# Nine equal chunks of 512 tokens in place of ten uneven ones, for windowed attention followed by a feed-forward layer

## The chip, the core and the metric

The kernel runs on one core of one Trainium2 chip. The core has five engines that run side by side, each with its own instruction list in program order: TensorE (PE in the profile; its weight loads are listed as PEld), VectorE (DVE), ScalarE (ACT), GpSimd (POOL) and SyncE (SP), which here issues the DMA transfers. Matrix products are accumulated in PSUM, everything else lies in SBUF. The metric is the device time of one execution in microseconds, as the median of the runs.

## The reference

Eight batches of eight heads, 576 positions and head size 64 go through causal attention in a window of 128 positions, with a distance penalty that has a slope of its own per head. The result, 4608 tokens of 512 numbers, goes through two matrix products with a piecewise function between them.

```python
scores = scale * np.matmul(q, k.transpose(0, 1, 3, 2))
rel = pos[:, None] - pos[None, :]
mask = (rel >= 0) & (rel < window)                    # window = 128
scores = np.where(mask, scores + bias[None], -1000000000.0)
attn = np.exp(scores - np.max(scores, axis=-1, keepdims=True))
attn = attn / (np.sum(attn, axis=-1, keepdims=True) + 1e-09)
x = np.matmul(attn, v)                                # to (4608, 512)
h = x @ w_in                                          # (512, 2048)
g = np.where(h >= 1, h, np.where(h <= -1, 0.0, (h + 1) ** 2 / 4))
return g @ w_out                                      # (2048, 512)
```

The two weight matrices arrive as 64-bit floats. The kernel makes 32-bit floats of them on the chip.

## The kernel before

**Chunks and stages.** The 36 blocks of 128 tokens are worked off in ten chunks (`SIZES`, ten numbers: 2, eight times 4, 2). For each chunk there is an attention stage, eight heads one after the other, and a feed-forward sweep over eight groups `g`; group `g` makes the hidden columns `g` and `8+g`, each of 128. While the sweep of chunk c runs, the attention of chunk c+1 is woven into it.

**Attention of one head** (`scores`, `weights_t`, `values`): products of queries and keys into PSUM tiles `s` (L544, L548 with plain float32; L550, L551 with operands split in two), then on DVE a selection by distance (L557) and a pass that adds the penalty and takes the row's bound (L560), on ACT the exponential (L564), on DVE or ACT the division by the row's sum (L575, L573), on PE the transposition `p` (L591), a copy to SBUF on ACT or DVE, on POOL two triangular selections per tile (L607, L610 or L622, L625), on PE the products with v into `x` (L659) and the copy into `xn`. Heads of chunks below `LIGHT` = 3 use plain float32 on PE; the others split q, k, v and the weights of attention into a rounded part and a rest of type fp32r, and multiply the parts.

**The feed-forward sweep.** Products in fp32r take three matmuls per pair of operands: high by high, high by rest, rest by high. In chunks 1 to 8 the first layer uses seven products of half-size quarters in place of eight (`PRODUCTS`, L722), with sums S1 to S4 of the weights' quarters A11 to A22 and differences T of the tokens' quarters. `build` (L387) splits each such operand once, during chunk 1, and writes it to DRAM; `fetch` (L397) reads it back in later chunks into a ring of ten buffers. The sums S are made by `operand` on POOL or, where the planner likes it better, on DVE (L380, L381). Chunk 9, of two blocks, uses eight plain products. The nonlinear function (`nonlinear`, L729) is a clamp on DVE, a square on ACT and a maximum on DVE, then a rounding on ACT (L744) and a rest on DVE (L745). The second layer (`layer2`) adds three fp32r matmuls per block and hidden column into `acc` (L762 to L764).

**Chunk 0** has a sweep of its own (`first_sweep`): both layers run in plain float32 on PE (L918 and L757), with weights just converted. During it the 32 halves of the weights are read and converted (`fetch_raw`, `convert`: two passes on ACT, L345 and L355, and two on DVE, L350 and L358), and split for later (`split_out`).

**What sets the order.** All operations are recorded first with their dependences. `Plan.schedule` (L119) is a list scheduler: it simulates the five engines with a table of costs and takes, on each engine, the ready operation that is due first; due times (`deadlines`) come from the order in which PE's operations were recorded. `emit` then writes the instructions in the planned order, so each engine's list is fixed when the kernel is built. Buffers with one slot in the pools (`buf`) add dependences: a tile that takes over a slot waits for the last use of the one before. The output tiles `o` have two slots.

Of the kernel before, what the change touches and what calls it, by code (L numbers as in the profile page):

```python
# [31 lines left out]
RAW_IN = ("B11", "B21", "T2", "T1", "B22", "T3")  # L32


class Buf:


    def __init__(self, name, make, before):
        self.name, self.make, self.before, self.tile = name, make, before, None
        self.nodes, self.writers, self.readers = [], {}, {}  # L40
        self.over = False
# [8 lines left out]
class Node:  # L50
    def __init__(self, alts, deps):
        self.alts, self.deps = alts, deps
        self.next, self.late, self.start, self.end, self.eng = [], None, None, None, None


class Plan:


    CROSS, SAME = 0.09, 0.04

    def __init__(self):
        self.nodes, self.slots, self.turn = [], {}, {}

    def buf(self, pool, tag, n, shape, dtype, name):
        k = self.turn.get(tag, 0)
        self.turn[tag] = k + 1
        slot = f"{tag}{k % n}"
        b = Buf(name, lambda: pool.tile(shape, dtype, name=name, tag=slot), self.slots.get(slot))
        self.slots[slot] = b
        return b  # L70

    def op(self, alts, reads=(), writes=()):
# [24 lines left out]
        for b, _ in reads + writes:  # L97
            b.nodes.append(node)
# [6 lines left out]
    def deadlines(self):  # L105
# [5 lines left out]
        for n in reversed(self.nodes):  # L111
            late = n.nominal if "PE" in n.alts else t + 5.0
            for s in n.next:
                late = min(late, s.late - min(a[1] for a in n.alts.values()) - self.CROSS)
# [3 lines left out]

    def schedule(self, engines, bandwidth):  # L119
        self.deadlines()  # L120
        free = {e: 0.0 for e in engines}
# [5 lines left out]
        tick = 0  # L127

# [18 lines left out]
        while events:  # L147
# [3 lines left out]
            cands = [(n.late, n.index, n, r) for n, r in avail[e] if r <= t + 1e-9]  # L151
# [3 lines left out]
            pick = None  # L155
            for late, _, n, r in cands:
                busy = n.alts[e][0]
                worse = [(m, q) for m, q in avail[e] if q > t + 1e-9 and q < t + busy - 0.05 and m.late < late - 0.2
# [8 lines left out]
            if pick is None:  # L167
                wake(e, min(q for _, q in avail[e] if q > t + 1e-9))
                continue
            n = pick  # L170
# [37 lines left out]
def windowed_attention_then_ffn(  # L208
# [14 lines left out]
    P = 128  # L223
# [4 lines left out]
    SIZES = [2] + [4] * 8 + [2]  # L228
# [6 lines left out]
    LIGHT = 3  # L235
    FIRST = 2
# [31 lines left out]

    def pool(t, f):
# [14 lines left out]
    half = const.tile([P, 1], F32, name="half")  # L284
    G.memset(half, 0.5)
    loaded = const.tile([P, 1], F32, name="loaded")
    S.activation(loaded, half, AF.Exp)
# [39 lines left out]
    def convert(i):
        fc, n = WEIGHTS[i]
        r = raw.pop(i)
        if fc not in w_of:  # L330
            w_of[fc] = buf("wp", "w", NFC + 1, [P, 2, DM], F32, f"w{fc}")
        w = w_of[fc]
# [7 lines left out]
        def o():  # L340
            return w.t[:, n].bitcast(I32)
# [15 lines left out]
        plan.op(dve_fast(DM, shift), [(r, 1)], [(w, n)])  # L357
        plan.op(dve(DM, lambda: V.tensor_tensor(o(), o(), low(), ALU.add), True), [(r, 0), (w, n)], [(w, n)])  # L358

    def split_out(fc):  # L360
        f = w_of[fc]
        w = wo_of[fc] = buf("wp", "w", NFC + 1, [P, 2, DM], F32R, f"wo{fc}")
        plan.op(act(DM, lambda: S.copy(w.t[:, 0], f.t[:, 1])), [(f, 1)], [(w, 0)])
        plan.op(dve(DM, lambda: V.tensor_tensor(w.t[:, 1], f.t[:, 1], w.t[:, 0].bitcast(F32), ALU.subtract), True),
                [(f, 1), (w, 0)], [(w, 1)])
# [3 lines left out]
    def operand(g, name):  # L369

        if name[0] == "A":
            w = w_of[g if name[1] == "1" else NG + g]
            k0 = 0 if name[2] == "1" else 2
            return w, 0, lambda: w.t[:, 0, k0 * P:(k0 + 2) * P].rearrange("p (c f) -> p c f", c=2)
        if (g, name) not in sums_w:
# [33 lines left out]
    def load_qk(p):  # L409
# [11 lines left out]
        other = c < LIGHT and p % 2  # L421
# [3 lines left out]
        kr = buf("ap", "kk" if other else "kr", 1, [P, 2, 5 * P], F32, f"kr_{p}")  # L425
        if c < LIGHT:
            st["kr"] = (kr, None, lambda: kr.t[:, 0])
            plan.op(dma(P * (n + P) * 4, lambda: DMA.dma_start(kr.t[:, 0, :n + P], k[rows, t0 - P:t0 + n])), (), [kr])
            return
        st["kr"] = (kr, None, lambda: kr.t[:, :, :n + P])  # L430
        for r in lo_rows:
            plan.op(dma(P * (n + P) * 4, lambda r=r: DMA.dma_start(
                kr.t[r, :, :n + P], k[rows, t0 - P:t0 + n].rearrange("(j d) t -> d j t", j=2))), (), [(kr, r.start)])

    def load_v(p):
        c, g = divmod(p, NPAIR)
        nb, b0 = SIZES[c], STARTS[c]
        if c == 0:
            if g % 2 == 0:
                t = pair[p]["v2"] = buf("ring", "r", 10, [P, 2, nb, P], F32, f"vn_{p}")  # L440
            else:
                t = pair[p - 1]["v2"]
            pair[p]["vn"] = (t, g % 2, lambda: t.t[:, g % 2])
            plan.op(dma(P * nb * 512, lambda: DMA.dma_start(t.t[:, g % 2], v[g, :, :nb])), (), [(t, g % 2)])
            return
        if c < LIGHT and p % 2:
            t = buf("ap", "vs", 1, [P, 2, 5, P], F32, f"vn_{p}")
            pair[p]["vn"] = (t, None, lambda: t.t[:, 0])
# [6 lines left out]
    def prepare_q(p):  # L455
# [3 lines left out]
        if c == 0:  # L459
            ql = buf("ring", "r", 10, [P, 2, n], F32, f"ql_{p}")  # L460
# [5 lines left out]
        for j in range(2):  # L466
            if c < LIGHT:
                plan.op(act_fn(n, lambda j=j: S.activation(ql.t[:, j, :n], qr(), AF.Copy, scale=qscale[:, g, j:j + 1])),
                        [(b, key)], [(ql, j)])
# [13 lines left out]
    def prepare_k(p):  # L483
# [4 lines left out]
        b, key, kr = pair[p]["kr"]  # L488
        kk = pair[p]["kk"] = buf("ap", "kk", 1, [P, 2, 5 * P], F32R, f"kk_{p}")
        kl = pair[p]["kl"] = buf("ap", "kl", 1, [P, 2, 5 * P], F32R, f"kl_{p}")  # L490
        for j in range(2):
            plan.op(act(n, lambda j=j: S.copy(kk.t[:, j, :n], kr()[:, j])), [(b, key)], [(kk, j)])
            plan.op(dve(n, lambda j=j: V.tensor_tensor(kl.t[:, j, :n], kr()[:, j], kk.t[:, j, :n].bitcast(F32),
                                                       ALU.subtract), True), [(b, key), (kk, j)], [(kl, j)])
# [18 lines left out]
    def att_bank(c, name):  # L513
        turn[0] += 1
        if c < FIRST and turn[0] % 2:
            return bank("acc1", 2, name)
        return bank("pa", 2, name)

    def scores(m, blks):
# [4 lines left out]
        if m not in head:  # L524
            z = buf("fp", "sw", 4, [P, 2, P], F32, f"z_{m}") if c == 0 else buf("ap", "z", 2, [P, 4, P], F32, f"z_{m}")
# [478 lines left out]
```

## Time and profile before

| What | us |
|---|---|
| median of 3 runs (1008.35 to 1009.16) | 1008.95 |
| the profiled execution | 1009.93 |
| its span from first to last instruction | 1008.1 |
| PE busy in it | 995.6 |
| DVE / ACT / POOL busy in it | 798.4 / 709.9 / 209.6 |
| data moved by DMA | 198.04 MB |

The page cuts the span into 40 slices of 25.2 us. PE is busy 9 tenths or more in every slice but the first (7) and the last (8). DVE has 6 tenths in the first slice, 8 or 9 in the next nine, 7 to 9 up to the 33rd, and falls after that; ACT has 9 in the second slice and 6 to 8 in nearly all others up to the 35th. From 230 us to 860 us the profile repeats every 105 us, which is one chunk of four blocks. In the tables below, a matmul that reads plain float32 is listed as two instructions, so 64 such matmuls show as x128.

### The profile page before, as it was taken

The page shows a single profiled execution, that of the slowest core. Times are in us where ns is not written, and L with a number is a line of the kernel's source. Part 1 is how long each engine was busy: PE and PEld are TensorE (multiplying, and loading weights), DVE is VectorE, ACT ScalarE, POOL GpSimd, SP SyncE. Part 2 cuts the span into 40 slices and gives each one's busy share as a digit, 9 for nine tenths or more (in the row PEclk, how much of TensorE's full clock was granted, in tenths as well). Part 3 has the DMA queues.
Part 4 walks back from the last instruction along what each step waited for, and adds up shares of the span by engine and source line. Part 5 has one row for each costly group of instructions (what it writes and reads, how often), then busy time and mean ns, then how long its engine had stood idle before and what let it go on. Part 6 is the DMA issues. An engine that isn't in the chain of part 4 may idle for free.

```text
span 1008.1 us, 19663 instructions
## 1 busy us (share of the span) xinstructions
PE 995.6 (99%) x6432; PEld 896.5 (89%) x6432; DVE 798.4 (79%) x2102; ACT 709.9 (70%) x1827; POOL 209.6 (21%) x319
## 2 busy tenths in 40 slices
PE   7999999999999999999999999999999999999998
PEld 6777799999999999999999999999999999999897
DVE  6899898999777987798779877897789778766443
ACT  7987788767777776777777777777778666754433
POOL 3231133403211221122112211121122221211000
PEclk9899999999999999999999999999999999999999
DMA  8596356567766677658664966576667655764471
GB/s 293 178 353 232 94 191 206 182 208 203 219 189 186 186 232 189 185 172 261 190 187 155 270 175 188 184 235 182 193 195 219 195 169 180 220 196 151 122 229 63
DMA packets 101909, 198.04 MB, mean 196 GB/s; under 512 B 11312, under 2 KB 14896, under 8 KB 101808
## 3 DMA queue, kind: packets, MB, share of 16 engines
q1 hardware_dynamic: 101808, 196.78, 64.3%
q8 instruction: 52, 0.85, 0.3%
q14 instruction: 49, 0.40, 0.1%
HBM read 170.52 MB, written 26.21 MB: 195 GB/s over the span
## 4 chain that ended last, share of the span: by engine, by line
PE 98%; ACT 1%; DVE 0%; issue 0%; POOL 0%; POOLq 0%; ACTq 0%
PE hA L722 18%; PE hB L722 14%; PE acc L762 13%; PE acc L763 13%; PE acc L764 12%; PE x L659 9%; PE p L591 3%; PE s L548 3%; PE h L918 3%; PE acc L757 3%; PE s L550 2%; PE s L551 2%; PE h L722 2%; PE idle L932 0%; PE s L544 0%
## 5 line engine op out<-in xcount | busy, mean ns | idle before, releaser
L762 PE MATMUL acc<-wo,gh 128*128 128x512 f32 x544 | 219.6, 404 | 0.0
L763 PE MATMUL acc<-wo,gh 128*128 128x512 f32 x544 | 214.6, 395 | 0.0
L764 PE MATMUL acc<-wo,gl 128*128 128x512 f32 x544 | 213.3, 392 | 0.0
L622 POOL TENSOR_SCALAR_AFFINE_SELECT lu<-lu 128x512 fp32r<-128x512 f32 (+1 forms) x112 | 79.6, 710 | 578.4 <-ACT lu L615 571.0
L735 ACT ACTIVATE m<-m,half 128x512 f32<-128x512 f32 (+1 forms) x160 | 108.6, 679 | 39.7 <-DVE m L732 24.6
L564 ACT ACTIVATE z<-z,nmax 128x128 f32<-128x128 f32 x288 | 112.7, 393 | 25.3 <-DVE nmax L560 25.1
L764 PEld LDWEIGHTS acc<-wo,gl 128*128 128x128 f32 x544 | 102.2, 188 | 23.6 <-DVE gl L745 0.2
L855 DVE TENSOR_TENSOR h<-hB,s 128x256 f32<-128x256 f32 x192 | 80.7, 420 | 46.9 <-PE hB L722 22.6
L762 PEld LDWEIGHTS acc<-wo,gh 128*128 128x128 f32 x544 | 102.8, 189 | 9.3 <-ACT gh L744 0.4
L763 PEld LDWEIGHTS acc<-wo,gh 128*128 128x128 f32 x544 | 103.1, 190 | 8.3
L745 DVE TENSOR_TENSOR gl<-h,gh 128x512 fp32r<-128x512 f32 x128 | 93.8, 733 | 16.8 <-ACT gh L744 15.4
L860 ACT COPY s<-hA 128x256 f32<-128x256 f32 x192 | 70.4, 367 | 49.3 <-PE hA L722 46.4
L722 PEld LDWEIGHTS hA<-x_T,w_S 128*128 128x128 f32 x672 | 93.7, 189 | 8.0
L744 ACT CAST gh<-h 128x512 fp32r<-128x512 f32 x128 | 79.2, 619 | 29.7 <-DVE h L738 28.4
L722 PE MATMUL hA<-x_T,w_S 128*128 128x256 f32 x672 | 99.2, 283 | 0.0
L738 DVE TENSOR_TENSOR h<-h,m 128x512 f32<-128x512 f32 x128 | 89.1, 696 | 2.2 <-ACT m L735 2.1
L557 DVE COPY_PREDICATED s<-older,s 128x256 f32<-128x256 uint32 x144 | 60.7, 422 | 23.4 <-PE s L551 15.6
L733 DVE TENSOR_SCALAR m<-h 128x512 f32<-128x512 f32 x128 | 55.3, 432 | 29.9 <-ACT h L866 27.5
L866 ACT COPY h<-hA 128x256 f32<-128x256 f32 x64 | 23.8, 372 | 73.6 <-PE hA L722 73.4
L560 DVE CUSTOM_DVE_ANT_0 z<-s,rel 128x128 f32<-128x128 f32 x288 | 72.2, 284 | 2.0
L625 POOL TENSOR_SCALAR_AFFINE_SELECT lu<-lu 128x512 fp32r<-128x512 f32 (+1 forms) x112 | 72.4, 669 | 0.0
L659 PEld LDWEIGHTS x<-lu,vs 128*128 128x128 f32 x528 | 67.5, 189 | 1.9
(127 smaller groups left out, 2169.4 us busy)
## 6 DMA issues: line engine op xcount, KB each, us to landing
w_S<-d_S SPq DMA_DIRECT2D x224, 256.0 KB, 2.7
w_A<-d_A SPq DMA_DIRECT2D x200, 256.0 KB, 3.0
kr<-in_k_dram SPq DMA_DIRECT2D x57, 320.0 KB, 4.8
vn<-in_v_dram SPq DMA_DIRECT2D x33, 320.0 KB, 3.3
out_dram<-o SPq DMA_DIRECT2D x36, 256.0 KB, 4.0
qr<-in_q_dram SPq DMA_DIRECT2D x33, 256.0 KB, 4.7
raw<-in_moe_w_in_dram SPq DMA_DIRECT2D x16, 512.0 KB, 6.0
raw<-in_moe_w_out_dram SPq DMA_DIRECT2D x16, 512.0 KB, 5.2
```

Source lines behind the costliest of these rows:

```text
L564: plan.op({"ACT": (0.385, 0.48, lambda i=i: S.activation(z.t[:, i], z.t[:, i], AF.Exp, bias=nmax.t[:, i:i + 1], scale=-1.0, accum_out=sm.t ...
L622: G.affine_select(out=lu.t[:, s, 0:2 * nb:2], in_=a.bitcast(F32), pattern=[[0, nb], [-1, P]], base=0, channel_multiplier=1, compare_op=ALU ...
L659: T.matmul(px[:, q0 * P:q1 * P], sv, mv.rearrange("p a w -> p (a w)"), start=(w == 0), stop=(w == len(todo) - 1), skip_group_check=True)
L722: T.matmul(o.t[:, :2 * P], w.t[:, a, kb], x.t[:, b, kb], start=start and n == 0, stop=stop and n == len(todo) - 1, skip_group_check=True)
L735: plan.op(act_fn(n, lambda: S.activation(m.t[:, :n], m.t[:, :n], AF.Square, bias=half[:, 0:1], scale=0.5)), [m], [m])
L738: plan.op(dve(n, lambda: V.tensor_tensor(f.t[:, :n], h.t[:, :n], m.t[:, :n], ALU.max), not h_ps), src + [m], dst)
L744: plan.op(act(n, lambda: S.copy(gh.t[:, :n], f.t[:, :n])), dst, [gh])
L745: alts = dve(n, lambda: V.tensor_tensor(gl.t[:, :n], f.t[:, :n], gh.t[:, :n].bitcast(F32), ALU.subtract), True)
L762: T.matmul(a.t, gh.t[:, ts], w.t[:, 0], start=first, stop=False)
L763: T.matmul(a.t, gh.t[:, ts], w.t[:, 1], start=False, stop=False)
L764: T.matmul(a.t, gl.t[:, ts], w.t[:, 0], start=False, stop=last)
L855: plan.op(dve(2 * P, lambda: V.tensor_tensor(f.t[:, key * 2 * P:(key + 1) * 2 * P], b.t[:, :2 * P], s.t, ALU.add)), [b, s], [(f, key)])
```

## The change

The tokens are cut into nine chunks of four blocks. Chunk 0 becomes a full chunk: its attention (eight heads of four blocks, plain float32, `LIGHT` = 2) stands ahead of all feed-forward work, its first layer uses the eight plain fp32r products per group on two halves of the tokens, and its second layer uses float32 matmuls for the hidden columns of groups 0 to 5 (`WHOLE` = 6) and three fp32r matmuls for groups 6 and 7. All split operands, the sums S among them, are now built during chunk 0; the sums are made on DVE alone. Chunks 1 to 8 use the seven products. The nonlinear function takes another form: max(h+1, 0), squared after halving, and a last step min(max(h, 1), that); its first step and all roundings may go to ACT or DVE, as the planner chooses. Several one-slot buffers are split in two (`kr`, `kk`, `lu`), weight halves share a common set of 17 slots that the planner hands out, and the planner runs twelve rounds, in each of which the due times are taken from the round before (`later`), and keeps the round whose plan ends first.

```diff
-    CROSS, SAME = 0.09, 0.04
+    CROSS, SAME, BACKLOG, STRETCH, SWAP, ROUNDS = 0.09, 0.04, 4.0, 1.5, 8.0, 12
...
+        for _ in range(self.ROUNDS):
+            order = self.forward(engines, bandwidth)
+            end = max(n.end for n in order)
+            if best is None or end < best[0]:
...
+            self.later(order)
...
-    SIZES = [2] + [4] * 8 + [2]
+    SIZES = [4] * 9
...
-    LIGHT = 3
-    FIRST = 2
+    LIGHT = 2
+    FIRST = 1
+    WHOLE = 6
...
+    def rounded(n, out, src):
+
+        alts = act(n, lambda: S.copy(out(), src()))
+        alts.update(dve_fast(n, lambda: V.tensor_copy(out(), src())))
+        return alts
...
-            alts = pool(0.75, lambda: G.tensor_tensor(s.t, af(), bf(), alu))
-            alts.update(dve(2 * P, lambda: V.tensor_tensor(s.t, af(), bf(), alu), True))
-            plan.op(alts, [(ab, ak), (bb, bk)], [s])
+            plan.op(dve(2 * P, lambda: V.tensor_tensor(s.t, af(), bf(), alu), True), [(ab, ak), (bb, bk)], [s])
...
-        if c < FIRST and turn[0] % 2:
-            return bank("acc1", 2, name)
+        if c < FIRST and turn[0] % 3:
+            return bank(f"acc{turn[0] % 3 - 1}", 2, name)
...
+    def nonlinear(c, fc, h, src, f):
+
+        n, psum = 4 * P, f is not h
+        m = buf("fp", "m", 2, [P, n], F32, f"m_{c}_{fc}")
+        alts = (dve if psum else dve_fast)(n, lambda: V.tensor_scalar(m.t, h.t, 1.0, 0.0, ALU.add, ALU.max))
+        alts.update(act(n, lambda: S.activation(m.t, h.t, AF.Relu, bias=one[:, 0:1]), 0.144 if psum else 0.186))
+        plan.op(alts, src, [m])
+        plan.op(act_fn(n, lambda: S.activation(m.t, m.t, AF.Square, scale=0.5)), [m], [m])
+        dst = [f] if psum else src
+        plan.op(dve(n, lambda: V.scalar_tensor_tensor(f.t, h.t, 1.0, m.t, ALU.max, ALU.min), not psum), src + [m], dst)
...
+        if c == 0 and fc % NG < WHOLE:
+            w, g, key = fo[fc % NG], gs[c, fc], fc // NG
+            plan.op(pe(0.858, lambda: T.matmul(a.t, g.t[:, ts], w.t[:, key], start=first, stop=False)), [g, (w, key)], [a])
...
+            if c == 0 and x == "A22":
+                for name in SUMS:
+                    build(g, name)
...
+            def plain(i, tt, st=st, g=g):
...
+                for kk in range(2):
+                    w = PLAIN[2 * i + kk]
+                    product(h, have[c, g, w], xs[c, f"B{kk + 1}{tt + 1}"], kk == 0, kk == 1, 2 * tt * P)
...
+            if c == 0:
+                for i, tt in ((0, 0), (0, 1), (1, 0), (1, 1)) if g < NG - 1 else ((0, 0), (1, 0), (0, 1), (1, 1)):
+                    steps.append([lambda plain=plain, i=i, tt=tt: plain(i, tt)])
...
-    while at[0] < ready[1]:
-        emit_attention(at[0] + 1)
-        if at[0] > ready[1] // 3 and converted[0] < EARLY:
-            weights_upto(converted[0] + 1)
-    weights_upto(EARLY)
+    emit_attention(ready[1])
+    operands_upto(AHEAD)
+    for fs in tokens_ready(0).values():
+        for f in fs:
+            f()
...
-    plan.emit(tc, ("PE", "ACT", "DVE", "POOL", "SP"), 270e3)
+    plan.emit(tc, ("PE", "ACT", "DVE", "POOL", "SP"), 370e3)
```

**First place: PE where the feed-forward of chunk 0 begins.** The rows give line, operation, output tile, operand tiles, columns and count. `s_4_..` is a score tile of head 8 and on (`kr_4` is the first pair of chunk 1), `p` a transposition, `x` the products with v, `h` a hidden column. Before, the eight heads of two blocks are all done, and then float32 products on whole tokens follow:

```order
L659 MATMUL x_7_456<-gh_7_428,vn_2_166 128x128
L659 MATMUL x_7_456<-gl_7_439,vn_2_166 128x128
L659 MATMUL x_7_456<-gh_7_428,vn_2_166 128x128
L918 MATMUL h_0_0_466<-xn_0_265,w0_336 128x256 x4
L548 MATMUL s_8_0_487<-kr_4_249,ql_4_397 128x256 x2
L548 MATMUL s_8_2_502<-kr_4_249,ql_4_397 128x256 x2
L548 MATMUL s_9_2_511<-kr_4_249,ql_4_397 128x256 x2
L918 MATMUL h_0_8_524<-xn_0_265,w8_414 128x256 x4
```

In the changed kernel the same place, after eight heads of four blocks (`x_0_B21` is the quarter of the tokens that needs the last four heads, `b_0_A12` a split quarter of the weights of group 0), reads:

```order
L774 MATMUL x_7_629<-gh_7_586,vn_3_197 128x128
L664 MATMUL s_9_2_651<-kr_4_263,ql_4_340 128x256 x2
L774 MATMUL x_8_659<-lu_8_637,vn_4_324 128x128 x8
L837 MATMUL h0_0_0_577<-x_0_B21_657,b_0_A12_473 128x256 x6
L837 MATMUL h0_0_0_577<-x_0_B12_478,b_0_A11_471 128x256 x6
L707 MATMUL p_9_703<-ident_78,z_9_618 128x128 x4
L664 MATMUL s_10_0_711<-kr_5_247,ql_5_529 128x256 x2
L837 MATMUL h1_0_0_723<-x_0_B11_460,b_0_A21_646 128x256 x6
```

Scores of heads 8 and 9, and the whole of head 8, have moved ahead of the first product that needs all of chunk 0's tokens.

**Second place: ACT at the same point.** `x_0_B21` is the rounding of that quarter, `xn_0` the tokens of chunk 0, `raw` a weight half under conversion:

```order
L451 ACTIVATE raw_5_392<-raw_5_392 128x512
L782 COPY xn_0_313<-x_6_602 64x512
L720 COPY lu_8_637<-p_8_621 128x512
L680 ACTIVATE z_9_618,sum_9_641<-z_9_618,nmax_9_619 128x128 x2
L359 CAST b_0_A22_649<-w_0_429 128x256
L782 COPY xn_0_313<-x_7_629 64x512
L359 CAST x_0_B21_657<-xn_0_313 128x512
L359 CAST x_0_B22_671<-xn_0_313 128x512
```

Before, chunk 0 needed no rounding of its tokens: behind the last copy into `xn_0` ACT went on with conversions.

**Third place: the end of ACT's list.** Before, two output tiles leave the core at the end:

```order
L744 CAST gh_9_7_13231<-g_9_7_13226 128x256
L735 ACTIVATE m_9_15_13244<-m_9_15_13244,half_83 128x256
L744 CAST gh_9_15_13255<-g_9_15_13253 128x256
L769 COPY o_9_0_13265<-acc_9_0_12821 128x512
L769 COPY o_9_1_13268<-acc_9_1_12837 128x512
```

Now there are four, and the roundings `gh` of the last columns stand on DVE:

```order
L851 ACTIVATE m_8_7_13116<-m_8_7_13116 128x512
L849 ACTIVATE m_8_15_13140<-h1_8_7_13101,one_83 128x512
L851 ACTIVATE m_8_15_13140<-m_8_15_13140 128x512
L885 COPY o_8_0_13175<-acc_8_0_12445 128x512
L885 COPY o_8_1_13181<-acc_8_1_12455 128x512
L885 COPY o_8_2_13187<-acc_8_2_12469 128x512
L885 COPY o_8_3_13190<-acc_8_3_12485 128x512
```

The last two copies take over the slots of the first two.

More of the change, by code (lines that the diff above doesn't have):

```diff
@@ L31 @@
 PLAIN = ("A11", "A12", "A21", "A22")
[L32 removed]
+SUMS = ("S1", "S2", "S3", "S4")
 class Buf:
@@ L97, in op @@
         for b, _ in reads + writes:
-            b.nodes.append(node)
+            if b.tag and not b.nodes:
+                node.need = b
+            if node not in b.nodes[-1:]:
+                b.nodes.append(node)
+                node.uses.append(b)
         node.deps.discard(node)
@@ L127, in schedule, with room @@
         tick = 0
+        slots = {tag: [(0.0, i) for i in range(n)] for tag, (n, _) in self.common.items()}
+        for _, bufs in self.common.values():
+            for b in bufs:
+                b.slot, b.left, b.last = None, len(b.nodes), 0.0
+        def room(n, t):
+            b = n.need
+            if b is None:
+                return True
+            free = sum(x <= t + 1e-9 for x, _ in slots[b.tag])
+            return free > 0 and b.fits(free)
         def wake(e, t):
@@ L167, in schedule @@
             if pick is None:
-                wake(e, min(q for _, q in avail[e] if q > t + 1e-9))
+                soon = [q for _, q in avail[e] if q > t + 1e-9]
+                wake(e, min(soon + [t + 0.2] if held_back else soon))
                 continue
+            if e == "DVE" and pick.alts[e][3] and lock["POOL"] > t + 0.15:
+                for late, _, n, r in cands:
+                    if not n.alts[e][3] and late < pick.late + self.SWAP and next(iter(n.alts)) == e:
+                        pick = n
+                        break
             n = pick
@@ new lines, in tokens @@
+            def tokens(n, g=g):
+                if g == NG - 1 and c + 1 < NCHUNK:
+                    for f in tokens_ready(c + 1).get(n, ()):
+                        f()
+            def plain(i, tt, st=st, g=g):
+                if i not in st:
+                    st[i] = bank("hB" if i else "hA", 1, f"h{i}_{c}_{g}")
+                h = st[i]
+                for kk in range(2):
+                    w = PLAIN[2 * i + kk]
+                    product(h, have[c, g, w], xs[c, f"B{kk + 1}{tt + 1}"], kk == 0, kk == 1, 2 * tt * P)
+                    if tt:
+                        used(c, g, w)
+                if tt:
+                    tag = ("gh", 4) if g < WHOLE else ("h", 3)
+                    nonlinear(c, i * NG + g, h, [h], buf("fp", *tag, [P, 4 * P], F32, f"g_{c}_{i * NG + g}"))
@@ new lines, in sweep_steps @@
+            if c == 0:
+                for i, tt in ((0, 0), (0, 1), (1, 0), (1, 1)) if g < NG - 1 else ((0, 0), (1, 0), (0, 1), (1, 1)):
+                    steps.append([lambda plain=plain, i=i, tt=tt: plain(i, tt)])
+                    for n in {(1, 0): (0, 1, 3), (1, 1): (4, 5, 6)}.get((i, tt), ()):
+                        steps[-1].append(lambda tokens=tokens, n=n: tokens(n))
+                    steps += [[second]] * 2
+                steps[-1].append(lambda g=g: weights_upto(4 * g + 4))
+            else:
```

413 lines of the change are left out of this document (214 added, 199 removed).

## The prediction

> **What bounds the kernel now.** I read the page first, its busy times and the chain of work that ended last:
>
> ```profile
> PE 995.6 (99%) x6432; PEld 896.5 (89%) x6432; DVE 798.4 (79%) x2102; ACT 709.9 (70%) x1827; POOL 209.6 (21%) x319
> ...
> PE 98%; ACT 1%; DVE 0%; issue 0%; POOL 0%; POOLq 0%; ACTq 0%
> ```
>
> PE is busy for 99% of the span, and 98% of the chain is PE. So I asked in which stretch PE is not busy, with the table of busy times by stage (us of the stage, then busy us and count of each engine, granted clock, DMA share, GB/s):
>
> ```profile
> 20.00:30.00 10.00, 5.48 (x32) 4.44 (x32) 8.93 (x27) 9.52 (x24) 5.38 (x9) 0.85 0.84 284
> ...
> 60.00:90.00 30.00, 30.00 (x139) 22.33 (x138) 28.16 (x79) 25.03 (x60) 8.91 (x10) 1.00 0.95 337
> ...
> 335.00:440.00 105.00, 105.00 (x706) 96.39 (x705) 85.08 (x220) 77.22 (x199) 22.51 (x34) 1.00 0.70 199
> ```
>
> PE waits only in the first 30 us. From 60 to 90 us DVE is busy 28.16 of 30 and DMA at 0.95, and PE still misses nothing. So two things decide: how much PE work there is, and what PE loses at the start and at the very end.
>
> **PE work.** While PE never waits, the pieces of the chain give the time from one matmul to the next (start, length, what, count; a plain float32 matmul counts as two):
>
> ```profile
> 30.12 3.41 PE h L918 x8
> ...
> 36.37 1.73 PE h L918 x8
> ...
> 41.13 1.73 PE s L548 x8
> ...
> 42.85 0.86 PE acc L757 x2
> ...
> 45.01 1.78 PE x L659 x16
> ```
>
> ```profile
> 121.20 0.44 PE p L591 x4
> ```
>
> ```profile
> 385.91 0.71 PE hA L722 x6
> ...
> 388.04 0.23 PE acc L762
> ...
> 389.44 1.11 PE x L659 x10
> ```
>
> One float32 matmul of 256 columns takes 1.73/4 = 0.432, one of 512 takes 0.86, one of 128 in the values 1.78/8 = 0.2225; in fp32r, 256 columns take 0.71/6 = 0.119 and 512 take 0.232 (0.23 rounded; three in a row take 0.69 to 0.70); a transposition 0.11; the values of one split head 1.11. The float32 stage that goes:
>
> ```profile
> L918 PE MATMUL h<-xn,w 128*128 128x256 f32 x128 | 32.0, 395 | 0.0
> ...
> L757 PE MATMUL acc<-w,g 128*128 128x512 f32 x64 | 31.6, 592 | 0.0
> ```
>
> By counting both programs:
> - First layer in float32: 64 matmuls go, 64 x 0.432 = -27.7.
> - Plain products of chunk 0 come (384), those of chunk 9 go (192); the other 2688 stay: +192 x 0.119 = +22.8.
> - Second layer in float32: 32 become 48 (six groups, two columns, four blocks): +16 x 0.86 = +13.7.
> - Second layer in fp32r: 3 x 544 become 3 x 528: -48 x 0.232 = -11.1.
> - Attention: `LIGHT` falls from ten blocks to eight. 16 float32 scores (-6.9) and 32 float32 values (-7.1) go, 32 split scores (+3.8) come; eight split heads of two blocks become whole ones, 1.11 in place of about 0.64 (four matmuls of 0.1, two of 0.119): +3.8.
>
> Sum: **-8.7 us** of PE work. This is the firm term: it rests on counts and on times without a wait.
>
> **The start.** PE's first scores, and what stands around its waits (start, length, engine; in brackets the idle time before and who ended it; then two stages):
>
> ```profile
> 5.33 0.85 PE s L544 x4
> ...
> 10.54 0.71 PE s L544 x4
> ```
>
> ```profile
> 28.47 0.79 PE L659 MATMUL x<-gh,vn 128*128 128x128 f32 x2 [2.16 <-POOL gh L610]
> ```
>
> ```profile
> 21.00:24.00 3.00, 1.40 (x10) 0.95 (x8) 2.89 (x15) 2.96 (x12) 0.89 (x3) 1.00 0.73 271
> 24.00:27.00 3.00, 1.54 (x8) 1.02 (x8) 2.71 (x6) 2.98 (x7) 2.21 (x4) 1.00 0.88 265
> ```
>
> Before, PE's own work between 5.33 and the first product of the feed-forward at 30.12 is 16 x 0.355 (L544) + 8 x 0.432 + 16 x 0.11 + 24 x 0.2225 = 16.3, so 8.5 of these 24.8 us are lost: ACT is busy 2.96 and 2.98 of 3 and PE half. On top, the first eight products take 3.41 in place of 1.73, at half clock: 1.7 lost. Together 10.2.
>
> The order of the changed kernel has, ahead of the first product that needs all tokens of chunk 0 (`x_0_B21`), 64 values, 36 transpositions, 32 scores of 256, 16 of 128 and six fp32r products: 14.2 + 4.0 + 13.8 + 5.7 + 0.7 = 38.4 of PE work. PE alone would get there at 5.33 + 38.4 = 43.7. ACT's list up to the rounding of that quarter, at ACT's own times from one start to the next:
>
> ```profile
> 60.23 1.32 ACT L468 ACTIVATE ql<-qr,qscale 128x512 f32<-128x512 f32 x2
> 61.62 0.59 ACT L604 COPY gh<-p 128x512 f32<-128x512 f32 x1
> 62.10 0.51 ACT L735 ACTIVATE m<-m,half 128x256 f32<-128x256 f32 x1
> ...
> 63.08 0.69 ACT L355 ACTIVATE raw<-raw 128x512 int32<-128x512 uint32 x1
> 63.65 0.68 ACT L345 ACTIVATE raw<-raw 128x512 f32<-128x512 f32 x1
> ...
> 66.64 0.39 ACT L564 ACTIVATE z<-z,nmax 128x128 f32<-128x128 f32 x1
> ...
> 67.03 0.39 ACT L564 ACTIVATE z<-z,nmax 128x128 f32<-128x128 f32 x1
> ```
>
> From the first exponential on there are 38 exponentials at 0.39, 7 scalings of q at 0.61 (half of 1.32, less the overlap), 14 copies at 0.48, 9 conversion passes at 0.57, 3 roundings of 512 at 0.5 and 3 of 256 at 0.3 (both estimates, from the copy): 14.8 + 4.3 + 6.7 + 5.1 + 1.5 + 0.9 = 33.3. Where it began and ended before:
>
> ```profile
> 7.72 0.40 ACT L564 ACTIVATE z<-z,nmax 128x128 f32<-128x128 f32 x1 [2.33 <-DVE nmax L560]
> ...
> 30.15 0.37 ACT L667 COPY xn<-x 64x256 f32<-64x256 f32 x1 [0.55 <-PE x L659]
> ```
>
> That list of before sums to 19.4 in the same way and took 22.4, a factor of 1.155 for waits. So ACT gets to the quarter at 7.72 + 33.3 x 1.155 = 46.2, without waits at 41.0; the rest on DVE adds 0.7. I take **47**, the value nearest to the row of before; the bounds are 43.7 (PE alone) and a start that loses as much as before. The loss is then 47 - 5.3 - 38.4 = 3.3, with no stage at half clock, since PE would be busy 38.4 of 41.7 us. Gain: 10.2 - 3.3 = **-6.9**.
>
> [...]
>
> **Behind the start.** Per group of chunk 0, PE has 48 x 0.119 + 8 x 0.86 and a head of 3.9: 16.5 us. DVE's work beside it:
>
> ```profile
> L358 DVE CUSTOM_DVE_ANT_0 w<-raw,w 128x1024 uint16<-128x1024 uint16 x32 | 22.2, 696 | 0.5 <-ACT raw L355 0.2
> ...
> L350 DVE TENSOR_SCALAR w<-raw 128x512 int32<-128x512 int32 x32 | 15.9, 502 | 0.7 <-ACT raw L345 0.6
> ...
> L391 DVE TENSOR_TENSOR b_A<-w,b_A 128x256 fp32r<-128x256 f32 x32 | 15.1, 478 | 0.0
> ...
> L770 DVE COPY o<-acc 128x512 f32<-128x512 f32 x9 | 6.2, 690 | 1.4 <-PE acc L764 0.8 <-DMA out_dram<-o 0.6
> ```
>
> ```profile
> 60.15 0.42 DVE L391 TENSOR_TENSOR b_S<-S,b_S 128x256 fp32r<-128x256 f32 x1
> 60.49 0.68 DVE L358 CUSTOM_DVE_ANT_0 w<-raw,w 128x1024 uint16<-128x1024 uint16 x1
> ```
>
> Four conversions (1.2 each), eight rests (0.48), four sums (0.43, like the rests), two nonlinear steps per column (0.69 each), a head of 3.0 and some three roundings at 0.69 (no row shows a rounding on DVE; a float32 copy out of PSUM is the dearest neighbour) make 18.4 by listed durations. But a next instruction starts about 0.08 before the one before ends (60.15 to 60.49 for one of 0.42), which takes off 2.2, and part of the first steps go to ACT: 13 to 16 for 16.5. So the sums and splits hide behind PE, and POOL, relieved of the sums, is not waited for. I cost them at nothing, and at the rival's price if the cover is gone. DMA needs about 280 GB/s there; 337 passed without a wait. In all later chunks columns wait 7 us of PE work or more between their last product and their use, as before: nothing.
>
> **The end.**
>
> ```profile
> 1003.31 1.28 ACT L769 COPY o<-acc 128x512 f32<-128x512 f32 x2 [1.06 <-PE acc L764]
> ...
> 1003.57 0.40 PE L764 MATMUL acc<-wo,gl 128*128 128x512 f32 x1
> ```
>
> ```profile
> out_dram<-o SPq DMA_DIRECT2D x2, 256.0 KB, 2.0
> ```
>
> Before, the last matmul ends at 1003.97 and the span 4.1 later. Now four output tiles share two slots: the second leaves PE 1.4 ahead of the end, is copied (0.6) and lands 2.0 later, 1.3 behind PE's end; only then can the fourth be copied (0.6), land (2.0) and the program close (1.4, as before): 5.4. **+1.3.**
>
> **Sum.** 1009.93 - 8.7 - 6.9 + 1.3 = 995.6 for the profiled execution; it lay 1.0 over the median, so **994.6**.
>
> **Rivals.**
> - The clock drops once more at the start: PE waits in a changed order on new chains (POOL's selections of 512 columns). Price 1.7, as before: 996.3. Chance 0.13.
> - The start is no cheaper: PE still loses 10.2, since ACT's list is longer than assumed (DVE's rows shift roundings to it). 994.6 + 6.9 = 1001.5. For it: ACT is the engine that is full there. Chance 0.15.
> - DVE becomes the bound of chunk 0's sweep, because its instructions wait for others and lose their overlap: 18.4 - 16.5 = 1.9 for each of eight groups, +15: 1009.8. Against: 28.16 of 30 busy without a wait of PE. It begins to cost when DVE needs 1.3 times its spacing. Chance 0.10, mostly with a smaller price.
> - Slower: the loss at the start grows with the attention that stands there. Twice the blocks, twice the loss, clock included: 20.4 in place of 3.3, +17.1: 1011.7. It ends above the time before when the loss passes 19.7. For it: the chain scores, bound, exponential, division, transposition, selection, values is run through for every head with little else for PE. Against: six PSUM tiles serve it in place of four, and PE's share of the work rises. Chance 0.08.
> - The change moves nothing measurable, because new waits eat the work saved: 0.02.
>
> **How the numbers follow.** The forecast has 0.52, with its own range of 990 to 999. The range reaches from PE alone at the start and no cost at the end (994.6 - 3.3 - 1.3 = 990.0, less the spread of runs) to the start that is no cheaper with some 2 us of waits: **989.5 to 1003.5**. It leaves out most of the DVE rival and the slower one. A measurement of this kernel tells about 0.2% from no change, 2 us. Faster by more than that: 0.52 + 0.13 + 0.15 + 0.04 = 0.84; within: 0.07; slower: 0.09.
>
> **What would show it.** Right: PE's busy time near 984, first product with all tokens of chunk 0 near 47 us, a granted clock of 1.00 in every stage from 10 to 60 us, no wait of PE between 50 us and its last matmuls, a wait of the third and fourth copy of `o` for the DMA at the end. Wrong: PE idle in stages between 50 and 160 us behind DVE or ACT (third rival), or a first such product past 55 us (second and fourth).

## The result and the profile after

The changed kernel took 997.96 us (median of four runs, 997.62 to 1000.59) beside 1008.85 for the kernel before: a ratio of 0.9898, 95% interval 0.9881 to 0.9916. That is 10.9 us less; the forecast was 994.6, 14.3 less. Its profiled execution was the one of 1000.59, 2.6 us above the median, with a span of 998.8 us.

The page after, its busy times, and the chain of work that ended last, by engine and by line:

```profile
PE 985.4 (99%) x6448; PEld 884.8 (89%) x6448; DVE 809.2 (81%) x2121; ACT 652.3 (65%) x1606; POOL 186.7 (19%) x274
...
PE 82%; DVE 8%; DMA 4%; ACT 4%; issue 1%; SPq 0%; ACTq 0%; DVEq 0%
PE hA L837 18%; PE hB L837 14%; PE acc L878 12%; PE acc L879 12%; PE acc L880 12%; PE x L774 6%; DMA d_S<-b_S 4%; PE s L666 3%; PE s L667 3%; PE p L707 2%; ACT z L680 1%; DVE b_S L506 1%; DVE z L676 1%; DVE S L494 1%; DVE s L673 1%
```

PE is as full as before, yet the chain, 98% PE before, now runs through DVE, DMA and ACT for 16% of the span. One transfer stands out: `d_S<-b_S`, the write of a split sum, with 4% (some 40 us). The busy times by stage show where (columns as in the prediction):

```profile
24.00:27.00 3.00, 3.00 (x26) 2.88 (x25) 3.00 (x15) 3.00 (x13) 0.99 (x2) 1.00 1.03 406
...
60.00:90.00 30.00, 30.00 (x182) 23.82 (x181) 27.21 (x76) 26.82 (x58) 2.75 (x4) 1.00 0.85 281
90.00:120.00 30.00, 28.31 (x159) 20.82 (x158) 26.89 (x84) 21.84 (x55) 3.01 (x2) 1.00 0.83 281
120.00:160.00 40.00, 37.16 (x203) 27.14 (x204) 36.18 (x95) 23.55 (x57) 3.95 (x4) 1.00 0.67 225
```

The start is full (before, PE was busy 1.54 us from 24 to 27) and the clock is 1.00. From 90 to 160 us PE is idle for 1.7 + 2.8 us, in the sweep of chunk 0, where before it missed nothing:

```profile
90.00:120.00 30.00, 30.00 (x142) 22.00 (x140) 26.27 (x73) 19.82 (x49) 3.33 (x4) 1.00 0.29 95
120.00:160.00 40.00, 40.00 (x282) 37.33 (x280) 35.29 (x102) 32.50 (x97) 14.79 (x19) 1.00 0.56 190
```

For a full balance I took every matmul: the time from its start to the next one's, less its unhindered time from the prediction's rows (0.119, 0.232, 0.43 and so on). What is left over is called **extra time** below; it is booked where the next matmul starts. A float32 matmul whose two records lie on both sides of the 60 us mark moves up to 0.4 us from one row to the next.

| profiled execution, us | before | after | difference | forecast |
|---|---|---|---|---|
| PE's unhindered work | 986.2 | 977.6 | -8.6 | -8.7 |
| extra time up to 60 us | 11.3 | 2.8 | -8.5 | -6.9 |
| extra time from 60 to 170 us | -0.1 | 6.8 | **+6.9** | 0 |
| extra time behind 170 us | 4.8 | 4.8 | 0.0 | 0 |
| last matmul to the end of the span | 4.1 | 5.0 | +0.8 | +1.3 |
| sum | | | -9.3 | -14.3 |

The spans agree: 1008.1 - 998.8 = 9.3. The waits from 95 to 172 us (engine, line, waited for, us in total, times, longest) and ACT's timeline ahead of PE's largest wait there (start, length; in brackets the idle time before and who ended it):

```profile
ACT b_S L359 <- DMA d_S<-b_S: 9.4, 8, 3.0
...
DVE b_S L360 <- DMA d_S<-b_S: 4.0, 3, 2.1
...
PE s L666 <- ACT kk L607: 1.3, 1, 1.3
...
PE s L664 <- DVE xn L783: 1.2, 1, 1.2
```

```profile
138.54 0.41 ACT L359 CAST b_S<-S 128x256 fp32r<-128x256 f32 x1 [0.28 <-DMA d_S<-b_S]
141.91 0.40 ACT L359 CAST b_S<-S 128x256 fp32r<-128x256 f32 x1 [2.97 <-DMA d_S<-b_S]
...
144.40 0.40 ACT L359 CAST b_S<-S 128x256 fp32r<-128x256 f32 x1 [1.02 <-DMA d_S<-b_S]
...
148.07 0.72 ACT L607 CAST kk<-kr 128x640 fp32r<-128x640 f32 x1 [0.38 <-DMA d_S<-b_S]
```

A split of a sum goes into one of two tiles, `kk0` and `kk1`, and is written to DRAM from there; the next split into that tile waits until the write has landed. The same two tiles then take the keys of chunk 2 (L607), for which PE waits at 148 us. The keys and their rests hold PE directly for 2.1 us only (1.3 and 0.8); its other waits from 95 to 172 us, each 1.2 us or less, are for other results of DVE and ACT. The chain of waits from 100 to 152 us shows what stands behind those: 37.9% of it are writes of sums. Some of its pieces show the tiles working as a queue:

```profile
106.04 0.40 DVE b_S L506
...
106.47 2.01 DMA d_S<-b_S
...
111.32 4.28 DMA d_S<-b_S
115.60 0.02 issue
115.63 0.29 DVE b_S L360
...
119.37 6.80 DMA d_S<-b_S
```

```profile
d_S<-b_S SPq DMA_DIRECT2D x32, 256.0 KB, 3.0
```

(the last row: issues from 60 to 170 us, count, size, median us from issue to landing). There are 32 such splits, 16 in each tile, each about 0.4 (rounding) + 0.5 (rest) + 3.0 (write, the median) = 3.9 us: 62 us if nothing else delays them. The first begins at 61 us, so by this sum the tiles would be free for the keys at 123; with all else in the queues it was 148 and 156. PE was ready for those keys at 147.5.

### The profile page after: what moved, and what is told of

Its sections match the earlier page's. It is cut to its first block, busy times and chain, and to the rows that moved or that the text cites. A ratio compares the mean times of both kernels' runs of the same rounds, so it can differ in the third digit from the quotient of the medians.

```text
span 998.8 us, 19588 instructions
## 1 busy us (share of the span) xinstructions
PE 985.4 (99%) x6448; PEld 884.8 (89%) x6448; DVE 809.2 (81%) x2121; ACT 652.3 (65%) x1606; POOL 186.7 (19%) x274
## 4 chain that ended last, share of the span: by engine, by line
PE 82%; DVE 8%; DMA 4%; ACT 4%; issue 1%; SPq 0%; ACTq 0%; DVEq 0%
PE hA L837 18%; PE hB L837 14%; PE acc L878 12%; PE acc L879 12%; PE acc L880 12%; PE x L774 6%; DMA d_S<-b_S 4%; PE s L666 3%; PE s L667 3%; PE p L707 2%; ACT z L680 1%; DVE b_S L506 1%; DVE z L676 1%; DVE S L494 1%; DVE s L673 1%
## 5 line engine op out<-in xcount | busy, mean ns | idle before, releaser
L878 PE MATMUL acc<-wo,gh 128*128 128x512 f32 x528 | 210.3, 398 | 0.0
L879 PE MATMUL acc<-wo,gh 128*128 128x512 f32 x528 | 208.6, 395 | 0.0
L880 PE MATMUL acc<-wo,gl 128*128 128x512 f32 x528 | 206.7, 391 | 0.0
L738 POOL TENSOR_SCALAR_AFFINE_SELECT lu<-lu 128x512 fp32r<-128x512 f32 x112 | 83.2, 743 | 580.1 <-ACT lu L731 566.4
L837 PE MATMUL hA<-x_T,w_S 128*128 128x256 f32 x768 | 114.0, 284 | 0.0
L837 PEld LDWEIGHTS hA<-x_T,w_S 128*128 128x128 f32 x768 | 106.4, 189 | 8.1
L851 ACT ACTIVATE m<-m 128x512 f32<-128x512 f32 x144 | 90.5, 628 | 10.4 <-DVE m L848 9.2
L853 DVE SCALAR_TENSOR_TENSOR h<-h,m 128x512 f32<-128x512 f32 x128 | 90.3, 705 | 3.9 <-ACT m L851 3.7
L741 POOL TENSOR_SCALAR_AFFINE_SELECT lu<-lu 128x512 fp32r<-128x512 f32 x112 | 78.2, 721 | 0.0
L837 PE MATMUL h<-x_B,b_A 128*128 128x256 f32 x384 | 71.7, 324 | 0.1
L774 PE MATMUL x<-lu,vs 128*128 128x256 f32 (+1 forms) x560 | 71.1, 274 | 0.0
L848 DVE TENSOR_SCALAR m<-h 128x512 f32<-128x512 f32 x77 | 35.0, 454 | 41.0 <-ACT h L987 38.4
```

What stands on the lines that cost most here:

```text
L738: G.affine_select(out=lu[s].t[:, 0:2 * nb:2], in_=a.bitcast(F32), pattern=[[0, nb], [-1, P]], base=0, channel_multiplier=1, compare_op=ALU ...
L774: T.matmul(px[:, q0 * P:q1 * P], sv, mv.rearrange("p a w -> p (a w)"), start=(w == 0), stop=(w == len(todo) - 1), skip_group_check=True)
L837: T.matmul(o.t[:, at:at + 2 * P], w.t[:, a, kb], x.t[:, b, kb], start=start and n == 0, stop=stop and n == len(todo) - 1, skip_group_check ...
L851: plan.op(act_fn(n, lambda: S.activation(m.t, m.t, AF.Square, scale=0.5)), [m], [m])
L853: plan.op(dve(n, lambda: V.scalar_tensor_tensor(f.t, h.t, 1.0, m.t, ALU.max, ALU.min), not psum), src + [m], dst)
L878: T.matmul(a.t, gh.t[:, ts], w.t[:, 0], start=first, stop=False)
```

## The experiments

In each set the kernel before ran on the same chip, and the medians are read against that. Extra time and end are those of the profiled executions.

| kernel | median, us | before, us | ratio (95%) | extra to 60 | 60-160 | 160-170 | end |
|---|---|---|---|---|---|---|---|
| changed, again | 998.56 | 1008.82 | 0.9893 (0.9880-0.9907) | 2.3 | 2.6 | 1.2 | 5.0 |
| sums staged in `gl` | 993.88 | 1008.82 | 0.9849 (0.9835-0.9862) | 2.6 | 0.0 | 0.1 | 5.0 |
| sums made on POOL | 997.25 | 1008.82 | 0.9884 (0.9869-0.9898) | 4.4 | 0.1 | 0.1 | 5.0 |
| last `o` in `z` | 997.30 | 1008.82 | 0.9879 (0.9866-0.9893) | 2.8 | 4.2 | 1.1 | 3.6 |
| `gl` and `z` | 993.47 | 1009.91 | 0.9837 (0.9822-0.9851) | 2.3 | 0.4 | 1.6 | 3.6 |
| two `gl` tiles only | 995.82 | 1009.91 | 0.9862 (0.9847-0.9877) | 2.8 | 0.5 | 1.5 | 5.0 |
| four PSUM tiles | 999.17 | 1009.91 | 0.9896 (0.9880-0.9913) | 2.8 | 4.2 | 0.6 | 5.0 |
| `gl`, `z`, `WHOLE` = 5 | 992.94 | 1009.91 | 0.9832 (0.9818-0.9847) | 2.3 | 0.1 | 1.4 | 3.6 |
| half in `kk`, half in `gl` | 995.96 | 1009.57 | 0.9864 (0.9849-0.9879) | 2.8 | 0.4 | 2.0 | 5.0 |
| planned with 270e3 | 1016.77 | 1009.57 | 1.0068 (1.0056-1.0081) | 2.9 | 0.1 | -0.1 | 5.0 |
| before, conversions held | 1010.42 | 1009.57 | 1.0008 (0.9999-1.0017) | 10.0 | 0.8 | 0.0 | 4.1 |
| `gl`, `z`, some sums on POOL | 993.62 | 1009.63 | 0.9846 (0.9833-0.9860) | 2.8 | 0.1 | 0.1 | 3.6 |

**The changed kernel again**, unaltered.

> The changed kernel once more, unaltered, beside the runs that follow. Every theory: a median of 997.6 to 998.5 us. PE's time beyond its own work between 60 and 170 us was about 7 us in the profiled execution of 1000.59; if that part hangs on when DMA transfers land, it differs between executions and is 4 to 7 here; if it comes from work that does not fit beside PE, it is 7 again within 0.5.

The part from 60 to 170 us was 3.8 us here and 6.8 in the first profile, with the same program. ACT and DVE waited 7.3 + 2.1 us for writes of sums between 95 and 172 us, then 9.4 + 4.0. So the loss moves together with these waits, which a fixed overload of an engine would not explain.

**The sums staged elsewhere.** `gl` has four tiles that hold nothing in the sweep until groups 6 and 7.

```diff
-            t = buf("ap", f"kk{SUMS.index(name) % 2}", 1, [P, 2, 2, P], F32R, f"b_{g}_{name}")
+            t = buf("fp", "gl", 4, [P, 2, 2, P], F32R, f"b_{g}_{name}")
```

> The split sums S are staged in the four gl tiles, which stand idle in the sweep of chunk 0, in place of the two kk tiles. Theory A (ACT and DVE stand behind a split that waits until the write of an earlier S has left its tile, 9.4 and 4.0 us between 95 and 172 us, and PE then waits for what is queued behind): these waits fall under 2 us, PE's extra time between 60 and 170 us falls from 4 to 7 us to 1 to 3, and the time is 3 to 5 us lower: 993 to 995. Theory B (DVE has too much work there): no wait of PE goes away but those for kk; 997 to 998. Theory C (transfers late because the DMA queue is full): the waits move to raw weights and the time stays within 1 us.

4.7 us less than the repeat. Its stages, and the shares of its chain of waits from 60 to 160 us:

```profile
60.00:90.00 30.00, 30.00 (x182) 23.82 (x181) 29.29 (x85) 29.93 (x67) 2.88 (x4) 1.00 0.96 342
90.00:120.00 30.00, 30.00 (x170) 22.45 (x170) 28.19 (x82) 24.00 (x57) 2.42 (x2) 1.00 0.84 296
120.00:160.00 40.00, 40.00 (x231) 30.56 (x230) 39.05 (x100) 25.64 (x61) 3.73 (x4) 1.00 0.63 209
```

```profile
by line: PE acc L871 39.5%; PE h L837 38.3%; PE x L774 10.7%; PE s L664 6.9%; PE p L707 2.3%; PE s L667 0.5%; PE s L666 0.5%; PE acc L878 0.5%; PE acc L879 0.5%; PE acc L880 0.5%
```

DVE is busier than in the changed kernel (29.29 of 30, 39.05 of 40) and PE waits for nothing: the chain is PE alone. So DVE's amount of work is not what stops PE. The waits for writes fell from 7.3 + 2.1 to 3.7 + 1.7, not under 2 as expected, and cost nothing.

**The sums on POOL again**, as in the kernel before.

```diff
-            plan.op(dve(2 * P, lambda: V.tensor_tensor(s.t, af(), bf(), alu), True), [(ab, ak), (bb, bk)], [s])
+            alts = pool(0.75, lambda: G.tensor_tensor(s.t, af(), bf(), alu))
+            alts.update(dve(2 * P, lambda: V.tensor_tensor(s.t, af(), bf(), alu), True))
+            plan.op(alts, [(ab, ak), (bb, bk)], [s])
```

> The sums S may be made on POOL again, as in the kernel before (31 of 32 then stand on POOL). Theory B: DVE is relieved of some 13 us between 50 and 160 us, PE's extra time there falls by 3 us or more, 993 to 995. Theory A: PE's extra time stays within 1.5 us of the changed kernel, since ACT and DVE still stand behind the two tiles; 997 to 999.

Here theory B's own sign came: the loss from 60 to 170 us is gone although the tiles are still shared. Only 1.3 us are won, since PE loses 2 us more ahead of 60 us (next row). Less work on DVE is thus a second way out: the queue through the tiles runs over DVE too, and kept its due time here, with the first keys rounded at 145.1 us and used at 147.4.

```profile
47.00:60.00 13.00, 11.74 (x83) 11.05 (x84) 11.51 (x33) 12.90 (x32) 2.60 (x4) 1.00 0.46 145
```

**Number of tiles or sharing?** Two tiles, but not those of the keys; then four, two of them shared.

```diff
+            plan.turn["gl"] = SUMS.index(name) % 2
+            t = buf("fp", "gl", 4, [P, 2, 2, P], F32R, f"b_{g}_{name}")
```

> The sums staged in two gl tiles only, so that the keys of chunk 2 have the kk tiles to themselves. If the number of staging tiles decides: ACT and DVE wait for the writes of S as in the unaltered changed kernel (9 us together), PE's extra time from 60 to 170 us stays at 2 us or more, and the time is 996 to 998. If it is the sharing of kk with the keys of chunk 2: the loss from 147 us on goes, the one at 104 to 120 us (1.1 in the repeat) stays, about 995.5. If neither: as the repeat, 998.5.

```diff
+            tag = ("fp", "gl", 4) if name in ("S3", "S4") else ("ap", f"kk{SUMS.index(name) % 2}", 1)
+            t = buf(*tag, [P, 2, 2, P], F32R, f"b_{g}_{name}")
```

> Four staging tiles for the sums, two of them still shared with the keys of chunk 2: S1 and S2 in the kk tiles, S3 and S4 in gl tiles. If the number of tiles is what matters, PE's extra time from 60 to 160 us is under 0.3 us, as with four gl tiles. If it is that the keys of chunk 2 stand behind the last sums in a shared tile, which draws all 32 splits ahead of other work, the first split of those keys still comes after 140 us, and PE loses 1 us or more between 140 and 160 us; with half the splits on each shared tile the loss may be smaller than in the unaltered changed kernel (3.0 and 4.6 us between 60 and 160 us in its two profiled executions gave 2.6 and 5.8).

With two tiles of their own the waits for writes are nearly as long as in the repeat, 7.8 + 1.0 us from 95 to 172 us in place of 7.3 + 2.1, but PE loses 0.5 us up to 160 in place of 2.6 (and 0.4 of the 0.5 is a matmul on the 60 us mark). The first keys of chunk 2 are rounded 52 us earlier than in the changed kernel, and PE is never idle from 120 to 160 us:

```profile
96.33 0.73 ACT L608 CAST kk<-kr 128x640 fp32r<-128x640 f32 x1
```

```profile
120.00:160.00 40.00, 40.00 (x227) 30.18 (x227) 37.88 (x94) 25.39 (x62) 3.55 (x4) 1.00 0.66 211
```

Both theories had the loss at 104 to 120 us stay; it went. The planner no longer draws the splits ahead of the weight conversions: the first rest of a sum comes at 72.7 us (61.8 in the changed kernel), and the last conversion pass starts at 112 us in place of 126. So up to 160 us it is the sharing, and not the number of tiles. With half of them shared (eight splits ahead of a key, not sixteen) the keys come at 126 and 144 us, in time, and PE loses 0.4 up to 160; that the first would still come after 140 was wrong. What is left at 160 to 170 us, 1.5 and 2.0 us, is not explained by this; the trace of the half-shared kernel puts 1.3 of it down to results of DVE (`lu` and `g`), and more on it stands below.

Each edit makes the planner draw up the whole order anew, so a new order alone might have removed the loss. It does not do so by itself: four PSUM tiles, or the last `o` in `z`, change the order and leave the sums as they are, and PE still loses 4.8 and 5.3 us from 60 to 170 us. Nor does sharing always cost: the plan with sums on POOL keeps it and loses 0.2 us there.

**Planned with the old bandwidth**, 270e3 in place of 370e3.

```diff
-    plan.emit(tc, ("PE", "ACT", "DVE", "POOL", "SP"), 370e3)
+    plan.emit(tc, ("PE", "ACT", "DVE", "POOL", "SP"), 270e3)
```

> The changed kernel, planned with a DMA bandwidth of 270e3 as before the change, in place of 370e3; nothing is computed differently. If the planner's belief that transfers land early is what puts waiting splits ahead of work that PE needs, PE's extra time from 60 to 170 us falls to 1 to 2 us and the time to 995 or less. If the shared tiles force that order whatever the plan assumes, it stays within 1.5 us of the repeat, 997 to 1000.

Neither: 7.2 us slower than the kernel before, where the repeat was 10.3 faster. The splits are now put later (the last at 177 us), and the keys stand behind them. The largest wait of PE from 5 to 180 us, and the chain up to it:

```profile
PE s L666 <- ACT kk L607: 8.5, 1, 8.5
```

```profile
172.16 0.44 DVE b_S L506
172.60 0.02 issue
172.61 2.70 DMA d_S<-b_S
175.32 0.02 issue
175.34 0.04 ACTq L607
175.37 0.04 issue
175.41 0.74 ACT kk L607
...
177.05 0.58 PE s L667
```

A write of a sum, the keys rounded into its tile, PE: the whole mechanism in one chain, with 22 us of extra time between 170 and 240 us and a mean granted clock of 0.90 from 160 to 230 us. So what the shared tiles cost, 2.6 to 5.4 us from 60 to 160 us in the changed kernel, hangs on when the plan ends the queue.

**The end.** For the last chunk, output tiles 2 and 3 go to the idle `z` tiles.

```diff
-            o = buf("fp", "o", 2, [P, DM], F32, f"o_{c}_{t}")
+            tag = ("ap", "z") if c == NCHUNK - 1 and t >= 2 else ("fp", "o")
+            o = buf(*tag, 2, [P, DM], F32, f"o_{c}_{t}")
```

> The last two output tiles of the last chunk go to the two z tiles, idle by then, in place of the slots of the first two. If the end is longer because the third and fourth copy wait for the DMA of the first two, the time from the last matmul to the end of the span falls from 5.0 to about 4.0 us, and the kernel by 1 us: 997. If that wait is hidden by PE's last matmuls anyway, nothing moves (998).

ACT's last copies in the changed kernel, then in this one:

```profile
991.82 1.27 ACT L885 COPY o<-acc 128x512 f32<-128x512 f32 x2 [4.92 <-PE acc L880]
994.57 1.27 ACT L885 COPY o<-acc 128x512 f32<-128x512 f32 x2 [1.48 <-DMA out_dram<-o]
```

```profile
990.45 2.62 ACT L886 COPY o<-acc 128x512 f32<-128x512 f32 x4 [4.92 <-PE acc L880]
```

The wait of 1.48 us for the write is gone and the end is 1.4 us shorter; the medians differ by 1.3.

**Both edits, and more on top.**

> The sums staged in the gl tiles and the last two output tiles in the z tiles, both at once. If the two losses are apart in the program, they add: 993.9 - 1.3 = 992.6 us, PE's extra time from 60 to 170 us under 0.3, the end 3.6 us behind the last matmul.

> The kernel with both edits, and group 5 of the second layer of chunk 0 in three fp32r matmuls too: eight float32 matmuls (0.86 each) go and 24 fp32r ones (0.232) come, 1.3 us less of PE work; DVE or ACT get two roundings and two rests of 512 columns more in the sweep of chunk 0. If PE's work still counts one to one and they hide: 1.3 below the kernel with both edits, 991.3. If DVE has no room left: PE waits between 100 and 170 us, and the time is not lower (992.6 or more).

> The kernel with both edits (gl staging, z tiles at the end), and the sums S of groups 2 to 7 allowed on POOL (22 of 24 then stand there); those of groups 0 and 1 stay on DVE, so that POOL's selections of the last heads of chunk 0 are not held up. With both edits PE still lost 1.5 us at 160 to 170 us, at the first product of chunk 1 and the heads beside it. If that is DVE's load, which falls by some 9 us ahead of it, the loss goes and the kernel is 1 us or more below the one with both edits (16.4 us below the kernel before): 17.5 or more below the kernel before. If it is something else (a transfer of chunk 1's first weights, the order of the transition), it stays at 1 us or more and the time within 0.7 us of that kernel; if POOL's sums hold up DVE's port or the selections, PE loses 1 us or more elsewhere.

Both edits: 16.4 us below the kernel before, where 10.3 (the repeat) and the two gains, 4.7 and 1.3, make 16.3. They add. Group 5 in fp32r (`WHOLE = 5`) takes 1.1 us off PE's busy time (984.0 to 982.9), but the medians, 17.0 and 16.4 below, don't tell the two apart. Both versions beat both kernels. What is left is a wait at the first product of chunk 1, which the trace of the kernel with both edits puts down to nothing that it shows:

```profile
163.05 0.95 PE L837 MATMUL hA<-x_B,w_A 128*128 128x256 f32 x6 [1.24 <-issue]
```

With sums of groups 2 to 7 on POOL this wait was gone (0.1 us), but PE lost 1 us more behind 170 us and the time stayed: 16.0 below, not the 17.5 expected. That POOL's sums held up DVE there is not shown: from 170 to 200 us DVE was busy for 28.40 us in 66 instructions, and for 29.06 us in 67 in the kernel with both edits. As the kernel staged in `gl` alone had no such wait either, at equal DVE work, its cause stays open.

**The start.** Four PSUM tiles for the attention of chunk 0 in place of six; and in the kernel before, conversions of later weights held back until the tokens of chunk 0 are there (`EARLY` = 2, and `held` in the reads of both ACT passes).

```diff
-        if c < FIRST and turn[0] % 3:
-            return bank(f"acc{turn[0] % 3 - 1}", 2, name)
+        if c < FIRST and turn[0] % 2:
+            return bank("acc1", 2, name)
```

> The changed kernel with four PSUM tiles for the attention of chunk 0 (pa and acc1, as the kernel before had) in place of six; no arithmetic changes. Theory S1 (the start is cheap because more tiles are in flight while ACT paces the chain): PE's extra time up to 60 us rises from 2.3 to 5 or more, and the time to 1001 or more. Theory S2 (it is cheap because a full chunk gives PE more work per exponential): within 1 us, 998 to 999.5, extra time at 60 us under 3.5.

```diff
+        held = [xn[0]] if 2 <= i < 12 else []
```

> The kernel before, with the weight conversions that its first products do not need (third half on) held back until the tokens of chunk 0 are done; they took eight passes of ACT, some 4.6 us, out of the 24.8 us ahead of the first product. Theory S2 (a chunk of two blocks gives PE too little work for the chain of each head): PE still loses 7 us or more of its 8.5 ahead of the first product, and the clock drops again. Theory S3 (the conversions crowd ACT): the first product comes about 4 us earlier, near 26 us, and the loss falls to 5 or less. The whole time may rise, since the conversions come later; only the start is read.

The tiles in flight make no difference: 2.8 us of extra time with four as with six. And in the kernel before, with conversions out of the way,

```profile
20.00:30.00 10.00, 6.66 (x35) 5.40 (x34) 7.91 (x27) 7.95 (x24) 5.15 (x10) 0.72 0.81 279
```

ACT is busy 7.95 of 10 us in place of 9.52, and PE still loses 9.4 us by 30 us (9.5 before); the clock drops as well, to a mean of 0.72 in this stage (0.85 before). Half clock came earlier and makes up 1.5 us of this loss, 0.6 before, so PE's waits alone are some 1 us shorter, and the first product starts at 29.78 us in place of 29.91. ACT's fullness between 20 and 30 us thus held PE for 1 us at most; from 10 to 20 us ACT was as full as before (9.39 of 10), so that part is not tested.

## Why the prediction was right in sign and 3.4 us too low

- **PE work, -8.7: right.** -8.6 by the matmuls' pace. The table of counts was the firm term that it was called.
- **The start, -6.9: right in direction, low by 1.6, and with the wrong reason.** The first product with all tokens came at 44.7 us, not 47:

```profile
42.93 2.00 PE L774 MATMUL x<-lu,vn 128*128 128x128 f32 x16
44.68 1.75 PE L837 MATMUL h<-x_B,b_A 128*128 128x256 f32 x12
```

  The step that was off is the factor of 1.155 on ACT's list, taken from the kernel before as if ACT paced the start. The held-back conversions show that with ACT less full between 20 and 30 us PE lost nearly as much; PE alone (43.7) was nearer. ACT began to round that quarter at 43.4 us (one such rounding takes 0.6), where the prediction had it done at 46.2. What remains is the other reading, that a chunk of two blocks gives PE too little work per pass through a head's chain. It fits both runs on the start, but is argued by taking its rivals away, not shown; that the number came near is in part luck.
- **Behind the start, "I cost them at nothing": the step that failed.** It cost 6.9 us in the profiled execution and 3.8 in the repeat. The prediction summed DVE's work per group and found room, 13 to 16 us for each 16.5; that holds, if narrowly, since with other staging tiles DVE is busy for 96.5 of the 100 us from 60 to 160 and PE waits for nothing. What it left out is the order: 32 splits that go one after another through two tiles, each waiting for a DMA write, with the keys of chunk 2 at the end. The rounding of 512 columns on DVE, taken as 0.69, was even cheaper, in the kernel with both edits:

```profile
159.53 0.42 DVE L360 CAST x_T<-xn 128x512 fp32r<-128x512 f32 x1
```

- **The third rival (DVE becomes the bound, +15)** named the place and allowed a smaller price, and the sign by which the prediction was to be seen wrong, PE idle between 50 and 160 us behind DVE or ACT, did come. (Its list of DVE's work adds up to 18.2, not 18.4, which makes its price 13.6.) Its mechanism, DVE's own sum of work, did not happen; that relief of DVE also cures the loss shows how near the two lie.
- **The end, +1.3:** +0.8 between the profiles, and 1.3 to 1.4 when it is taken away; the wait for the slots is as described.
- The rivals of a clock drop, a start no cheaper and a loss doubled at the start did not come: granted clock 1.00 in every stage from 10 to 990 us, extra time 2.8. That no stage of the start would run at half clock, which the term of -6.9 includes, was an estimate from two stages of the kernel before; PE was busy for 37.99 of the 39.37 us up to the first product with all tokens, at a clock of 1.00.

With the staging moved, the change is worth 14.9 us, against 14.3 forecast. So of the forecast's sum one zero was wrong, offset in part by the start, whose surplus of 1.6 us was luck.

## What to carry to other kernels

Room in an engine's sum of work does not show that a step is hidden. Where several producers share a tile that a DMA has to empty, multiply: uses of the tile times (make + write), from the first use on, and compare with the time at which the last user of that tile is due; here 62 us with the median write, in a stretch of 86. That it fits is not enough: it took 87 as it ran, among all else that the engines and the DMA queue had to do, and cost PE time, so the sum has to leave ample room. Lending a tile of the next stage as a staging tile puts that stage's first instruction at the end of the queue; it is safer to lend one whose owner comes late.

## What the runs showed of the hardware

The records of the granted clock in the kernel before: full for 20.48 us, up to 27.09 us from the span's start, then half for 6.83 us, then full for 972.80 us, up to 2.7 us behind the last matmul. In the 6 us from 21 to 27 us, ahead of the fall, PE was busy for 2.95 us, and its longest pause there, the one that the fall lies in, was 2.16 us. With the conversions held, the mean clock was 0.72 from 20 to 30 us, where PE was busy for 6.66 of 10 us, and 0.96 from 30 to 47; as an estimate from these two means, some 7 us of half clock. In the plan with 270e3 it was 0.90 from 160 to 230 us, with PE busy for 54.22 of 70.

In the changed kernel one record of full clock runs for 993.28 us, from 5.42 us to 4.9 us behind the last matmul. It holds a stretch, from 147.1 to 150.1 us, in which PE was busy for 0.84 of 3.0 us, with pauses of 1.33 and 0.83 us, less than in either half of the 6 us above (1.40 and 1.54 of 3). So a low busy share over 3 us did not bring the clock down each time, and what decides is not shown. In the other ten kernels and repeats the mean clock of the profiled execution was 0.999 or 1.000.
